# A decode kernel's layer norms: the columns centred only, the norm's factor applied behind the products, and x joined to the output amid w4's products

## The chip, the cores and the metric

The kernel runs on one core of one Trainium2 chip. The metric is device time in microseconds (us) of one execution; the time of a kernel is the median of its runs. Lower is better.

## The reference, cut to what matters

Two layers, each used twice: A is attention with a cache of keys and values for one new token, B a small network. Eight sequences (B = 8), width D = 448, 16 query heads on 8 key heads, 4096 cached positions, head width 256, hidden width F = 1792. All inputs are bf16.

```python
def _layernorm(x, axis=-1, eps=1e-5):
    m = jnp.mean(x, axis=axis, keepdims=True)
    v = jnp.var(x, axis=axis, keepdims=True)
    return (x - m) / jnp.sqrt(v + eps)

def _A_ref(x, k_cache, v_cache, wq, wo):
    q = (x @ wq).reshape(B, Sq, Hq, Dh).transpose(0, 2, 1, 3)
    ...                                   # k, v: each cache head serves two query heads
    p = _softmax(jnp.einsum("bhqd,bhkd->bhqk", q, k) * (Dh ** -0.5))
    o = jnp.einsum("bhqk,bhkd->bhqd", p, v)
    return o.transpose(0, 2, 1, 3).reshape(B, Sq, Hq * Dh) @ wo

def _B_ref(x, w1, w2, w3, w4):
    ...                                   # hs: four shifted parts of h, through w2
    x1 = x + hs
    h2 = _gelu(_layernorm(x1) @ w3) @ w4
    return x1 + h2

x = x + _A_ref(_layernorm(x), A_k_cache, A_v_cache, A_wq, A_wo)
x = x + _B_ref(_layernorm(x), B_w1, B_w2, B_w3, B_w4)
x = x + _A_ref(_layernorm(x), A_k_cache, A_v_cache, A_wq, A_wo)
x = x + _B_ref(_layernorm(x), B_w1, B_w2, B_w3, B_w4)
```

The sequence length is 1, so the four shifted parts of h are zero, hs is zero, and w1 and w2 play no part. B applied to a norm therefore holds two norms, one after the other: x1 is norm(x), and the columns for w3 are norm(norm(x)). Both have the same mean and variance behind them, so they differ by a factor per sequence.

## The kernel before

**The work.** Nearly all of the time goes into the caches: for each of two passes (the two uses of A), each sequence b and each pair of key heads gp, four blocks of keys and four of values of 1 MB each are loaded into one of 15 slots (`slots`, all parts of the tile `places`). A key block is transposed in place by VectorE (`transpose_k`, L713, three instructions), multiplied with the queries by TensorE (`scores`, L728), and the exponentials are taken by ScalarE (`exps`, L737). Values are multiplied by TensorE (`pv`, L783). Some blocks of the first pass stay in their slots for the second, some are parked in PSUM (`away`, `back`, L748 and L755). A key slot comes free when its scores are done, a value slot when its products are done; `emit_loads` then issues the next load on SP's queue, in an order fixed when the program is built.

**The order.** It is written out by hand (`manual_schedule`): one loop over the blocks (`items`), and in it, twice per block, `step(idx)`, which takes one piece of a generator that does the rest of the work of a sequence. A `yield` ends a piece. `add_gen` gives each generator the blocks between which it should run, and a number of pieces (`of`: 38 for `chain`, 23 for `rest`) by which `step` paces it. If the next pass needs a sequence's queries before its chain has ended, the loop takes pieces until they are there. On each engine the instructions run in the order in which they were written.

**The generators around the change.**

- `project_q(0, Bn, qT1)` runs alone at the start: the norm of all eight sequences, then the queries of the first pass with wq (L309). Its scratch is in `scratch`, that is, in the last slot.
- `chain(b)` follows the first pass of each sequence: output projection with wo (L358), `mlp(b, 1)` with w3 (L376) and w4 (L358), then `project_q(b, 1, qT)`, the queries of the second pass.
- `rest()` does the second pass's `mlp` for the first four sequences together.
- The last four sequences' second `mlp_hidden(MID, Bn - MID)` stands alone behind everything, followed by the output in rows: x goes through an identity into `o_row` in PSUM (L995, fp32, two matmuls of the trace for each in the program), the products with w4 are added to it (L1005), the sum is copied as bf16 (L1014) and stored (L1016).

**The norm.** x is held as columns, `xT`: 128 partitions x 4 blocks of D x sequences; the fourth block overlaps the third by 64 rows. `norm(x, nb, twice)` makes sums and sums of squares on VectorE (L220 to L223), adds over partitions with a matmul of ones (L228), copies the means (L231), makes the variance (L234, or L238 and L239), adds epsilon (L255, L261, L265), and lets GpSimd take the power -1/2 (`power`, L247). `twice` asks for two factors: `rs[:, 0]` for norm(x), `rs[:, 1]` for norm(norm(x)). For more than one sequence these are two instructions on GpSimd, the one for `rs[:, 1]` first. Then `xc` is x less its mean (L268), and `xb`, the bf16 columns for the products, is `xc` times the last factor (L276 and L284 for one sequence, three instructions of L286 for more: all rows of three blocks, and two halves of the fourth). With `twice`, x itself becomes x + norm(x) (L295, or L297 and L298).

**The gelu.** `mlp_hidden` halves the products out of PSUM (L394), makes the cubic (L395, L396), tanh on ScalarE (L397), and HT (L399), the columns for w4. In `project_q` the products are copied as they are (L318).

Of the kernel before, what the change touches and what calls it, by code (L numbers as in the profile page):

```python
# [11 lines left out]
ACT = mybir.ActivationFunctionType  # L12
ALU = mybir.AluOpType
EPS = 1e-5
# [3 lines left out]
def kernel(  # L18
# [27 lines left out]
    nc = tc.nc  # L46
    Bn, Sq, D = A_x.shape
# [10 lines left out]
    HC = F // 128  # L58
# [84 lines left out]
    low = consts.tile([128, 2, 4], FP32, name="low")  # L143
# [13 lines left out]
    def xbs(nb):  # L157
        return xb[1] if nb == 1 else xb[Bn][:, :, :nb]
# [18 lines left out]
    xT = consts.tile([128, 4, Bn], FP32, name="xT")  # L177
# [25 lines left out]
    def norm(x, nb, twice):  # L203

        def room(name, shape, at):
            n = shape[0] * shape[1]
            if nb < Bn:
                t = chn.tile([128, n * MID], FP32, tag=name)  # L210
                ap = t[:, 0 : n * nb]
            else:
                ap = scratch(at, n * nb)
            return ap.rearrange("p (s f b) -> p s f b", s=shape[0], f=shape[1])

        def bc(ap):
            return ap.unsqueeze(1).to_broadcast([128, 4, nb])

        xx = room("xx", (2, 4), 0)
        nc.vector.tensor_mul(xx[:, 0], x, wv[:].unsqueeze(2).to_broadcast([128, 4, nb]))  # L220
        nc.vector.tensor_mul(xx[:, 1], xx[:, 0], x)
        xs = room("xs", (1, 2), 512)[:, 0]
        nc.vector.tensor_reduce(  # L223
            xs, xx.rearrange("p s f b -> p s b f"), mybir.AxisListType.X, ALU.add
        )
        yield
        st = room_ps("st", nb).rearrange("p (s b) -> p s b", b=nb)
        nc.tensor.matmul(st, ones, xs, start=True, stop=True)  # L228
        yield
        mv = room("mv", (1, 2), 528)[:, 0]  # L230
        nc.vector.tensor_copy(mv, st)  # L231
        var = room("var", (1, 1), 608)[:, 0, 0]
        if nb == 1:
            nc.vector.scalar_tensor_tensor(  # L234
                var, mv[:, 0], mv[:, 0], mv[:, 1], ALU.mult, ALU.subtract, reverse1=True
            )
        else:
            nc.vector.tensor_mul(var, mv[:, 0], mv[:, 0])  # L238
            nc.vector.tensor_sub(var, mv[:, 1], var)  # L239


        ve = room("ve", (1, 2), 544)[:, 0]
        n = 2 if twice else 1
        rs = room("rs", (1, 2), 560)[:, 0]

        def power(k0, k1):
            nc.gpsimd.tensor_tensor(  # L247
                rs[:, k0:k1].rearrange("p n b -> p (n b)"),
                ve[:, k0:k1].rearrange("p n b -> p (n b)"),
                nhalf[:].to_broadcast([128, (k1 - k0) * nb]),  # L250
                ALU.pow,
            )

        if twice and nb == 1:
            nc.vector.scalar_tensor_tensor(  # L255
                ve[:, :, 0], var.to_broadcast([128, 2]), 0.0, eps2[:], ALU.max, ALU.add
            )
            power(0, 2)
        else:
            if twice:  # L260
                nc.vector.tensor_scalar(  # L261
                    ve[:, 1], var, 0.0, EPS * EPS / (1 + EPS), ALU.max, ALU.add
                )
                power(1, 2)
            nc.vector.tensor_scalar(ve[:, 0], var, 0.0, EPS, ALU.max, ALU.add)  # L265
            power(0, 1)
        xc = room("xc", (1, 4), 576)[:, 0]
        nc.vector.tensor_tensor(xc, x, bc(mv[:, 0]), ALU.subtract)  # L268
        yield
        if nb > 1:  # L270
            yield
        c = (1 + EPS) ** -0.5 if twice else 1.0
        rl = rs[:, n - 1]
        parts = ((0, 128, 0, 0, 3, 0), (0, 64, 64, 3, 4, 4), (64, 128, 64, 3, 4, 3))
        if nb == 1:
            nc.vector.scalar_tensor_tensor(  # L276
                xbs(1)[:, 0:4, 0], xc[:, :, 0], rl, low[:, int(twice)], ALU.mult, ALU.mult
            )
            parts = parts[1:2]
        for p0, p1, x0, f0, f1, to in parts:  # L280
            pp = slice(x0, x0 + p1 - p0)
            dst = xbs(nb)[p0:p1, to : to + f1 - f0, :]
            if nb == 1:
                nc.vector.tensor_scalar(dst, xc[pp, f0:f1], rl[pp], c, ALU.mult, ALU.mult)  # L284
            else:
                nc.vector.scalar_tensor_tensor(  # L286
                    dst,
                    xc[pp, f0:f1],
                    c,
                    rl[pp].unsqueeze(1).to_broadcast([p1 - p0, f1 - f0, nb]),  # L290
                    ALU.mult,
                    ALU.mult,
                )
        if twice and nb == 1:
            nc.vector.scalar_tensor_tensor(x, xc, rs[:, 0], x, ALU.mult, ALU.add)  # L295
        elif twice:
            nc.vector.tensor_tensor(xc, xc, bc(rs[:, 0]), ALU.mult)  # L297
            nc.vector.tensor_add(x, x, xc)  # L298
        yield

    def project_q(b0, nb, qT):

        yield from norm(xT[:, :, b0 : b0 + nb], nb, False)
        q_ps = room_ps("q", nb).rearrange("p (c b) -> p c b", b=nb)
        for j in range(2):
            for h in range(Hq):
                for fc in range(4):
                    w, xi = wblk(wq_sb, HD, 2 * h + j, fc)
                    nc.tensor.matmul(  # L309
                        q_ps[:, j * Hq + h, :],  # L310
                        w,
                        xbs(nb)[:, xi, :],
                        start=(fc == 0),
                        stop=(fc == 3),
                    )
                if h % 4 == 3:
                    yield
        nc.vector.tensor_copy(qT, q_ps)  # L318
        yield

    def spread_q(qT, qbd):
# [46 lines left out]

    def mlp_hidden(b0, nb):

        yield from norm(xT[:, :, b0 : b0 + nb], nb, True)
        h_ps = room_ps("h", nb)
        for c in range(HC):
            for fc in range(4):
                w, xi = wblk(w3_sb, F, c, fc)
                nc.tensor.matmul(  # L376
                    h_ps[:, c * nb : c * nb + nb],
                    w,
                    xbs(nb)[:, xi, :],
                    start=(fc == 0),  # L380
                    stop=(fc == 3),
                )
            if c % 4 == 3:
                yield
        yield
        g_t = chn.tile([128, 2, HC * MID], FP32, tag="g")
        hh, g0 = g_t[:, 0, 0 : HC * nb], g_t[:, 1, 0 : HC * nb]
        if nb == 1:
            HT_t = chn.tile([128, HC, 1], BF16, tag="HT")
            HT = HT_t[:]  # L390
        else:
            HT = HTw[:, :, b0 : b0 + nb]

        nc.vector.tensor_scalar_mul(hh, h_ps, 0.5)  # L394
        nc.vector.scalar_tensor_tensor(g0, hh, 2 * 0.044715, h_ps, ALU.mult, ALU.mult)  # L395
        nc.vector.scalar_tensor_tensor(g0, g0, 1.0, h_ps, ALU.add, ALU.mult)  # L396
        nc.scalar.activation(g0, g0, ACT.Tanh, scale=0.7978845608028654)  # L397
        yield
        nc.vector.scalar_tensor_tensor(  # L399
            HT,  # L400
            g0.rearrange("p (c b) -> p c b", b=nb),
            1.0,
            hh.rearrange("p (c b) -> p c b", b=nb),
            ALU.add,
            ALU.mult,
        )
        yield
        return HT

# [449 lines left out]
    for idx, it in enumerate(items):  # L859
        if idx == len(items) - 2:  # L860
            end = [slots[p] for p in places[:2]]
            ident2 = end[0][:, 0:256].bitcast(FP32)
            nc.vector.tensor_copy(ident2, identb[:])
            W = D // 4
            o_row = store[0][:, 0:W]
            nc.vector.memset(o_row, 0.0)
        n, kv, c = it
# [119 lines left out]
    xs = xT[:, :, MID:]  # L987
    nc.vector.tensor_add(xs, xs, st["y"])
    run(mlp_hidden(MID, Bn - MID))
    for q in range(4):  # L990
        for fc in range(4):
            at = min(128 * fc, D - 128)
            lo, hi = max(W * q, 128 * fc), min(W * q + W, at + 128)
            if lo < hi:
                nc.tensor.matmul(  # L995
                    o_row[32 * q : 32 * q + Bn, lo - W * q : hi - W * q],
                    xT[:, fc, :],
                    ident2[:, lo - at : hi - at],
                    start=(lo == W * q),
                    stop=False,  # L1000
                    skip_group_check=True,
                )
    for c in range(HC):
        for q in range(4):
            nc.tensor.matmul(  # L1005
                o_row[32 * q : 32 * q + Bn, :],
                HTw[:, c, :],
                w4_sb[:, c, W * q : W * q + W],
                start=False,
                stop=(c == HC - 1),  # L1010
                skip_group_check=True,
            )
# [36 lines left out]
```

## Time and profile before

| | |
|---|---|
| median of 3 runs | 1098.04 us |
| lowest and highest | 1095.36 and 1102.22 us |
| profiled execution: span | 1093.6 us |
| TensorE (PE) busy, weight loads (PEld) | 674.9 us, 451.8 us |
| VectorE (DVE) busy | 599.1 us |
| ScalarE (ACT), GpSimd (POOL) busy | 125.9 us, 16.3 us |
| mean rate of all transfers | 409 GB/s |
| read from HBM | 444.67 MB |
| mean granted clock of TensorE | 0.593 |

The span goes from the first to the last instruction of one profiled execution; the page gives no other time of that execution, so what lies around the span is seen only by comparing it with the runs. A line of the trace is read as start, length, engine, source line, operation, output and input, shapes, and in brackets how long the engine was idle before it and what ended that. SPq is SP's queue, on which the loads are issued. A busy share is an average over the whole execution: what a stretch is bound by is read from that stretch.

### The profile page before, as it was taken

What the parts mean: (1) busy time and instruction counts of PE and PEld (TensorE: products, weight loads), DVE (VectorE), ACT (ScalarE), POOL (GpSimd) and SP (SyncE); (2) the same over time, 40 slices, a digit from 0 to 9 for tenths busy, and PEclk for the clock granted to TensorE, in tenths of its full rate; (3) what the DMA queues carried; (4) which work ended last, traced back from release to release, by engine and by line L of the source; (5) the groups of instructions that cost most, each with busy time, mean ns of one, the idle gap of its engine ahead of it and who ended that gap; (6) DMA issues with size and microseconds to landing.
All of it is one profiled execution on the core that took longest, in us unless ns stands there. A gap on an engine that the chain in (4) does not pass through costs nothing. (4 is left out here: it accounts for less than half of the span.)

```text
span 1093.6 us, 32866 instructions
## 1 busy us (share of the span) xinstructions
PE 674.9 (62%) x15063; PEld 451.8 (41%) x15063; DVE 599.1 (55%) x1215; ACT 125.9 (12%) x362; POOL 16.3 (1%) x27
## 2 busy tenths in 40 slices
PE   3234568456864677446774467834776477767775
PEld 2123345334642355324552245522454244545554
DVE  4256564656366555555465564665637553585462
ACT  0001101110110111101021001201111101111110
POOL 0000000000000000000000000000000000000000
PEclk9986556655575556555566555665556555665565
DMA  9999999999999999999999999999999999999994
GB/s 356 394 427 419 416 403 420 420 416 407 418 423 419 406 417 422 423 419 402 419 422 423 420 401 418 423 421 417 411 416 421 420 398 419 421 411 409 421 417 188
DMA packets 62010, 446.80 MB, mean 409 GB/s; under 512 B 6568, under 2 KB 10544, under 8 KB 12336
## 3 DMA queue, kind: packets, MB, share of 16 engines
q1 hardware_dynamic: 61680, 444.32, 98.6%
q8 instruction: 118, 1.93, 0.7%
q10 hardware_dynamic: 192, 0.38, 0.2%
q14 instruction: 20, 0.16, 0.0%
HBM read 444.67 MB, written 0.01 MB: 407 GB/s over the span
## 5 line engine op out<-in xcount | busy, mean ns | idle before, releaser
L713 DVE STREAM_TRANSPOSE places<-places 128x512 uint32<-128x512 uint32 (+1 forms) x576 | 462.0, 858 | 263.1 <-DMA places<-in_A_k_cache_dram 262.7
L728 PE MATMUL sc<-places,qbd 128*8 128x128 bf16 (+1 forms) x6720 | 281.9, 309 | 217.8 <-DVE places L713 179.7
L783 PE MATMUL o<-places,ptw 128*8 128x256 bf16 x3968 | 241.9, 387 | 144.6 <-DMA places<-in_A_v_cache_dram 122.1
L728 PEld LDWEIGHTS <-qbd 128*8 128x8 bf16 x6720 | 161.2, 101 | 312.8 <-issue 136.8
L783 PEld LDWEIGHTS <-ptw 128*8 128x8 bf16 x3968 | 114.1, 109 | 192.2 <-issue 151.0
L737 ACT ACTIVATE p_n<-sc 128x256 bf16<-128x256 f32 x128 | 95.6, 747 | 763.1 <-PE sc L728 763.1
L309 PEld LDWEIGHTS <-wq_sb 128*128 128x128 bf16 x1152 | 36.0, 104 | 28.3 <-issue 18.4
L358 PEld LDWEIGHTS <-wo_sb 128*128 128x128 bf16 x1280 | 38.4, 102 | 19.8 <-issue 19.8
L332 DVE CAST qbd<-misc 32x64 bf16<-32x64 f32 x64 | 13.8, 216 | 55.6 <-PE misc L328 55.0
L309 PE MATMUL misc<-xb,wq_sb 128*128 128x1 bf16 x1024 | 34.5, 166 | 6.2 <-ACT ptw L771 3.2
L358 PE MATMUL misc<-OT,wo_sb 128*128 128x1 bf16 x1024 | 34.5, 165 | 1.2 <-issue 1.2
L737 ACT ACTIVATION_READ_ACCUMULATOR p_n<-sc 128x1 f32 x128 | 33.9, 265 | 0.0
L771 ACT CAST ptw<-misc 128x128 bf16<-128x128 f32 x64 | 17.4, 273 | 139.1 <-PE misc L764 79.1
L463 PEld LDWEIGHTS misc<-R,o_sb 128*128 128x128 f32 x124 | 26.1, 292 | 9.4 <-issue 8.6
L247 POOL TENSOR_TENSOR t<-t,nhalf 128x2 f32<-128x2 f32 (+2 forms) x20 | 14.0, 703 | 1064.9 <-DVE t L268 1064.9
L463 PE MATMUL misc<-R,o_sb 128*128 128x8 f32 x124 | 28.8, 342 | 0.1
L431 PE MATMUL misc<-zm,one 128*128 128x8 f32 (+1 forms) x66 | 18.5, 354 | 15.0 <-DVE zm L423 14.2
L755 DVE STREAM_TRANSPOSE places<-store 128x512 uint32<-128x512 uint32 x32 | 20.1, 684 | 10.7 <-PE sc L728 10.6
L431 PEld LDWEIGHTS misc<-zm,one 128*128 128x128 f32 x66 | 16.0, 300 | 21.5 <-issue 15.8
L376 PEld LDWEIGHTS <-w_sb 128*128 128x128 bf16 x560 | 17.2, 105 | 9.4 <-issue 9.2
L376 PE MATMUL misc<-xb,w_sb 128*128 128x1 bf16 (+1 forms) x560 | 18.5, 166 | 3.6 <-DVE xb L286 2.2
L748 DVE STREAM_TRANSPOSE store<-places 128x512 uint32<-128x512 uint32 x32 | 19.9, 690 | 0.9 <-DMA places<-in_A_v_cache_dram 0.8
(103 smaller groups left out, 241.9 us busy)
## 6 DMA issues: line engine op xcount, KB each, us to landing
places<-in_A_v_cache_dram SPq DMA_DIRECT2D x215, 1024.0 KB, 9.5
places<-in_A_k_cache_dram SPq DMA_DIRECT2D x146, 1024.0 KB, 9.9
places<-in_A_k_cache_dram SPq DMA_DIRECT2D x23, 2048.0 KB, 18.7
places<-in_A_v_cache_dram SPq DMA_DIRECT2D x8, 768.0 KB, 7.2
wo_sb<-in_A_wo_dram SPq DMA_DIRECT2D x1, 3584.0 KB, 27.5
wq_sb<-in_A_wq_dram SPq DMA_DIRECT2D x3, 1024.0 KB, 8.0
w_sb<-in_B_w_dram SPq DMA_DIRECT2D x1, 1568.0 KB
w_sb<-in_B_w_dram SPq DMA_DIRECT2D x3, 448.0 KB, 26.2
```

Source lines behind the costliest of these rows:

```text
L309: nc.tensor.matmul(q_ps[:, j * Hq + h, :], w, xbs(nb)[:, xi, :], start=(fc == 0), stop=(fc == 3),)
L358: nc.tensor.matmul(y_ps[:, fc, :], w[:, i, at : at + 128], rhs(i), start=start, stop=stop, skip_group_check=open is not None,)
L376: nc.tensor.matmul(h_ps[:, c * nb : c * nb + nb], w, xbs(nb)[:, xi, :], start=(fc == 0), stop=(fc == 3),)
L431: nc.tensor.matmul(z_ps, ones, zm[:], start=True, stop=True)
L463: nc.tensor.matmul(ot_ps[:, j], o_sb[:].rearrange("p (i j) -> p j i", j=2)[:, j], R[:], start=True, stop=True)
L713: nc.vector.transpose(w, w)
L728: nc.tensor.matmul(sc[32 * k : 32 * k + 8, 128 * x : 128 * (x + nx)], qbd[:, ep, gp].rearrange("p a h -> p (a h)"), v, start=(n == 0), sto ...
L737: nc.scalar.activation(p_sb[:, :, :, 2 * u : 2 * u + 2].rearrange("p t i x -> p x t i"), sc[:, 256 * u : 256 * u + 256].rearrange("p (x t ...
L748: nc.vector.transpose(store[n][:].bitcast(U32), slot[:].bitcast(U32)[:, 512 * n : 512 * n + 512])
L755: nc.vector.transpose(slot[:].bitcast(U32)[:, 512 * n : 512 * n + 512], store[n][:].bitcast(U32))
L771: nc.scalar.copy(ptw[:, :, :, 6:8], pt_ps.rearrange("p t k (a h) -> p a (t k) h", a=4),)
L783: nc.tensor.matmul(o_ps[32 * q : 32 * q + 8, :], ptz[:, at : at + 8], v[:, y * Dh : (y + 1) * Dh], start=False, stop=(y >= 12), skip_group ...
```

## The change

`norm` writes `xb` as soon as the means are there, as x less its mean without a factor, and ends a piece there; the variance and the powers follow in the next piece, at whose end `norm` returns. It returns the factor, and with `twice` also a function, `add_normed`, that makes x + norm(x); only for that is `xc` still made. A new function, `scaled`, applies the factor to the products when they are taken out of PSUM: in `project_q` in place of the copy, in `mlp_hidden` in place of the halving. The cubic is then made from the halved and scaled products in SBUF (with other constants) and not from the products in PSUM. `add_normed` runs after HT. A norm has three pieces instead of four (one sequence) or five (more); the paces are not changed. At the end, x's matmuls into `o_row` stand in front of the eighth of the 14 chunks of w4's products instead of before the first.

```diff
@@ norm
         mv = room("mv", (1, 2), 528)[:, 0]
         nc.vector.tensor_copy(mv, st)
+        parts = ((0, 128, 0, 0, 3, 0), (0, 64, 64, 3, 4, 4), (64, 128, 64, 3, 4, 3))
+        if nb == 1:
+            nc.vector.scalar_tensor_tensor(
+                xbs(1)[:, 0:4, 0], x[:, :, 0], mv[:, 0], low[:, 0], ALU.subtract, ALU.mult
+            )
+            parts = parts[1:2]
+        for p0, p1, x0, f0, f1, to in parts:
+            pp = slice(x0, x0 + p1 - p0)
+            dst = xbs(nb)[p0:p1, to : to + f1 - f0, :]
+            if nb == 1:
+                nc.vector.tensor_scalar(
+                    dst[:, :, 0], x[pp, f0:f1, 0], mv[pp, 0], None, ALU.subtract
+                )
+            else:
+                nc.vector.tensor_tensor(
+                    dst,
+                    x[pp, f0:f1],
+                    mv[pp, 0].unsqueeze(1).to_broadcast([p1 - p0, f1 - f0, nb]),
+                    ALU.subtract,
+                )
+        yield
         var = room("var", (1, 1), 608)[:, 0, 0]
...
-        xc = room("xc", (1, 4), 576)[:, 0]
-        nc.vector.tensor_tensor(xc, x, bc(mv[:, 0]), ALU.subtract)
-        yield
-        if nb > 1:
-            yield
...
-        yield
+        if twice:
+            xc = room("xc", (1, 4), 576)[:, 0]
+            nc.vector.tensor_tensor(xc, x, bc(mv[:, 0]), ALU.subtract)
+
+            def add_normed():
+                if nb == 1:
+                    nc.vector.scalar_tensor_tensor(x, xc, rs[:, 0], x, ALU.mult, ALU.add)
+                else:
+                    nc.vector.tensor_tensor(xc, xc, bc(rs[:, 0]), ALU.mult)
+                    nc.vector.tensor_add(x, x, xc)
+
+            return rs[:, 1], add_normed
+        return rs[:, 0]
+
+    def scaled(dst, ps, rs, factor, nb):
+
+        if nb == 1:
+            nc.vector.tensor_scalar(dst, ps, rs, factor, ALU.mult, ALU.mult)
+        else:
+            n = dst.shape[1]
+            nc.vector.scalar_tensor_tensor(
+                dst, ps, factor, rs.unsqueeze(1).to_broadcast([128, n, nb]), ALU.mult, ALU.mult
+            )
@@ project_q
-        nc.vector.tensor_copy(qT, q_ps)
+        scaled(qT, q_ps, rs, 1.0, nb)
@@ mlp_hidden
-        nc.vector.tensor_scalar_mul(hh, h_ps, 0.5)
-        nc.vector.scalar_tensor_tensor(g0, hh, 2 * 0.044715, h_ps, ALU.mult, ALU.mult)
-        nc.vector.scalar_tensor_tensor(g0, g0, 1.0, h_ps, ALU.add, ALU.mult)
-        nc.scalar.activation(g0, g0, ACT.Tanh, scale=0.7978845608028654)
+        scaled(
+            hh.rearrange("p (c b) -> p c b", b=nb),
+            h_ps.rearrange("p (c b) -> p c b", b=nb),
+            rs,
+            0.5 * (1 + EPS) ** -0.5,
+            nb,
+        )
+        nc.vector.scalar_tensor_tensor(g0, hh, 4 * 0.044715, hh, ALU.mult, ALU.mult)
+        nc.vector.scalar_tensor_tensor(g0, g0, 1.0, hh, ALU.add, ALU.mult)
+        nc.scalar.activation(g0, g0, ACT.Tanh, scale=2 * 0.7978845608028654)
         yield
         nc.vector.scalar_tensor_tensor(HT, ...)
+        add_normed()
         yield
@@ the output
+    def x_part():
+        ...                      # the loops over q and fc as before, with start=False
     for c in range(HC):
+        if c == HC // 2:
+            x_part()
         for q in range(4):
             nc.tensor.matmul(
                 o_row[32 * q : 32 * q + Bn, :],
                 HTw[:, c, :],
                 w4_sb[:, c, W * q : W * q + W],
-                start=False,
+                start=(c == 0),
                 stop=(c == HC - 1),
                 skip_group_check=True,
             )
```

More of the change, by code (lines that the diff above doesn't have):

```diff
@@ L266, in norm @@
             power(0, 1)
-        xc = room("xc", (1, 4), 576)[:, 0]
-        nc.vector.tensor_tensor(xc, x, bc(mv[:, 0]), ALU.subtract)
-        yield
-        if nb > 1:
-            yield
-        c = (1 + EPS) ** -0.5 if twice else 1.0
-        rl = rs[:, n - 1]
-        parts = ((0, 128, 0, 0, 3, 0), (0, 64, 64, 3, 4, 4), (64, 128, 64, 3, 4, 3))
+        if twice:
[10 more added lines that the diff above has]
+    def scaled(dst, ps, rs, factor, nb):
         if nb == 1:
+            nc.vector.tensor_scalar(dst, ps, rs, factor, ALU.mult, ALU.mult)
+        else:
+            n = dst.shape[1]
             nc.vector.scalar_tensor_tensor(
-                xbs(1)[:, 0:4, 0], xc[:, :, 0], rl, low[:, int(twice)], ALU.mult, ALU.mult
+                dst, ps, factor, rs.unsqueeze(1).to_broadcast([128, n, nb]), ALU.mult, ALU.mult
             )
[L279 to L298, printed above, removed]
-        yield
     def project_q(b0, nb, qT):
-        yield from norm(xT[:, :, b0 : b0 + nb], nb, False)
+        rs = yield from norm(xT[:, :, b0 : b0 + nb], nb, False)
         q_ps = room_ps("q", nb).rearrange("p (c b) -> p c b", b=nb)
@@ L369, in mlp_hidden @@
     def mlp_hidden(b0, nb):
-        yield from norm(xT[:, :, b0 : b0 + nb], nb, True)
+        rs, add_normed = yield from norm(xT[:, :, b0 : b0 + nb], nb, True)
         h_ps = room_ps("h", nb)
@@ L989 @@
     run(mlp_hidden(MID, Bn - MID))
[L990 to L1002, printed above, removed]
+    def x_part():
+        for q in range(4):
+            for fc in range(4):
+                at = min(128 * fc, D - 128)
+                lo, hi = max(W * q, 128 * fc), min(W * q + W, at + 128)
+                if lo < hi:
+                    nc.tensor.matmul(
+                        o_row[32 * q : 32 * q + Bn, lo - W * q : hi - W * q],
+                        xT[:, fc, :],
+                        ident2[:, lo - at : hi - at],
+                        start=False,
+                        stop=False,
+                        skip_group_check=True,
+                    )
     for c in range(HC):
+        if c == HC // 2:
+            x_part()
         for q in range(4):
```

## The prediction

> **What bounds the kernel now.** I read the page first, then the kernel cut into stretches of 10 us, then the end and the start in order of time, then the waits. "Faster" and "slower" below mean by over 1%, 11 us here: the three runs shown spread over 0.6%, so less than about 1% can hardly be told from no change. First the page's head, its engine row and its DMA rows:
>
> ```profile
> span 1093.6 us, 32866 instructions
> PE 674.9 (62%) x15063; PEld 451.8 (41%) x15063; DVE 599.1 (55%) x1215; ACT 125.9 (12%) x362; POOL 16.3 (1%) x27
> DMA  9999999999999999999999999999999999999994
> DMA packets 62010, 446.80 MB, mean 409 GB/s; under 512 B 6568, under 2 KB 10544, under 8 KB 12336
> ```
>
> No compute engine is above 62%; the DMA engines are at nine tenths or more in 39 of 40 slices, and the change touches no transfer. Next, three of the 10 us stretches (PE, PEld, DVE, ACT and POOL busy, then granted clock, DMA share, GB/s):
>
> ```profile
> 630.00:640.00 10.00, 8.22 (x170) 5.71 (x170) 5.71 (x13) 1.29 (x4) 0.00 (x0) 0.50 0.98 387
> ...
> 1070.00:1080.00 10.00, 7.60 (x230) 6.82 (x229) 1.62 (x10) 1.05 (x3) 0.00 (x0) 0.50 0.87 354
> 1080.00:1090.00 10.00, 5.12 (x152) 4.50 (x153) 3.46 (x21) 0.25 (x1) 1.99 (x2) 0.50 0.01 2
> ```
>
> The first is one of the poorest in the middle: even there the DMA share is 0.98, against 1.01 in the stretch 60 to 1080 us as a whole, at 416 GB/s. So compute is exposed only after the last load lands, at about 1080.7 us. That tail, in order of time (start, length, engine, line, idle time before it and what ended it):
>
> ```profile
> 1083.77 0.17 DVE L231 COPY t<-misc 128x8 f32<-128x8 f32 x1 [0.69 <-PE misc L228]
> ...
> 1084.36 0.17 DVE L261 TENSOR_SCALAR t<-t 128x4 f32<-128x4 f32 x1
> ...
> 1084.67 1.99 POOL L247 TENSOR_TENSOR t<-t,nhalf 128x4 f32<-128x4 f32 x2 [67.88 <-DVE t L268]
> 1085.72 0.55 DVE L286 SCALAR_TENSOR_TENSOR xb<-t 128x12 bf16<-128x12 f32 x3 [1.05 <-POOL t L247]
> 1085.95 1.74 PE L376 MATMUL misc<-xb,w_sb 128*128 128x4 bf16 x56 [2.22 <-DVE xb L286]
> ...
> 1087.62 0.58 PE L995 MATMUL store<-places,xT 128*8 128x112 f32 x14
> 1087.72 0.22 DVE L394 TENSOR_SCALAR g_t<-misc 128x56 f32<-128x56 f32 x1 [0.64 <-PE misc L376]
> ...
> 1088.75 0.22 DVE L399 SCALAR_TENSOR_TENSOR HTw<-g_t 128x56 bf16<-128x56 f32 x1 [0.32 <-ACT g_t L397]
> 1089.02 1.48 PE L1005 MATMUL store<-w_sb,HTw 128*8 128x112 bf16 x56 [0.83 <-DVE HTw L399]
> 1090.55 0.27 DVE L1014 CAST places<-store 128x112 bf16<-128x112 f32 x1 [1.59 <-PE store L1005]
> ```
>
> From the means (L231) to the products with w3 (L376) lie 2.2 us, nearly half of it GpSimd's first power. The x part (L995) runs while VectorE and ScalarE make the gelu, so it costs nothing now.
>
> **The change in the tail.** The sum is against the profiled execution's span, 1093.6 us, the only time of its own that the page has; the median of the runs, 1098.04, lies 4.4 us above it, and I carry the difference over.
>
> Products start earlier. The three centring operations follow L231 at once, at 1083.96 where the variance starts now. The three of L286 that they replace began 0.19 us apart, and PE started 0.23 us after the first (1085.72 to 1085.95), so PE now starts at 1084.19. It needs 1.77 us to VectorE's next start (1085.95 to 1087.72), plus about 0.1 us, once, for the half block that the second operation writes at about 1084.3: the products are done at about 1086.05.
>
> The factor comes later. The variance is pushed back by three operations, 3 x 0.19 = 0.57 us, so the first power starts at 1084.67 + 0.57 = 1085.24. From its start to VectorE's use 1.05 us passed (1084.67 to 1085.72), so the factor is there at 1086.29. Of the two, this is the later. The new scaling operation thus starts at 1086.29 and not, like L394, at 1087.72: 1.43 us gained. What replaces the wait for the power before the products is a wait of 0.24 us for it behind them. Behind it on VectorE stand the two operations of the cubic and HT; ScalarE waits for them.
>
> Scaling and gelu keep four operations on VectorE. The new form of the first (two tensor inputs, one from PSUM, 56 elements) is in no row of before as such; L395 has two tensor inputs, one from PSUM, at 0.214 us, L394 has one at 0.196. I take +0.02 us; its bounds are 0 and, by L318's 0.425 us for 256 elements, +0.2.
>
> The cubic's operations now run beside the second power. In this trace the three operations of L286, with two tensor inputs from SBUF, also ran under the second power, in 0.157 to 0.172 us each, against 0.162 for the same line's 64-row form at the start with GpSimd idle: no contention, and I take none. Against that stands the Trainium skill, GPSIMD Engine Reference, section Specifications: GpSimd's SBUF interface is shared with VectorE, and VectorE operations with two SBUF inputs contend for it. By that page the cubic would be held from 1086.54 to the power's end at about 1087.25, and the tail's sum would be -0.1 us instead of the one below.
>
> The x part moves onto the path. Its 14 matmuls took 0.58 us hidden under the gelu; now they stand after 28 of w4's 56 and lengthen that stretch by as much: +0.58 us (bounds +0.4 if weight loads overlap, +0.65). Its new input comes from two operations after HT: these are L297 and L298, 0.40 us from the first's start to the second's end, and need the second power, done at 1085.24 + 1.99 = 1087.23. HT ends at about 1087.57, x at about 1088.0; PE comes to the x part at 1087.62 + 28 x 0.0268 = 1088.37. So x has 0.37 us to spare; without that cover the wait would be added one for one.
>
> Sum: -1.43 + 0.02 + 0.58 = -0.83 us.
>
> **The change at the start.** The first projection loses its wait for the power (1.64 us on GpSimd), but the next rows show that the products wait for wq:
>
> ```profile
> 7.80 0.57 DVE L286 SCALAR_TENSOR_TENSOR xb<-places 128x24 bf16<-128x24 f32 x3 [1.67 <-POOL places L247]
> 9.54 0.19 PE L309 MATMUL store<-xb,wq_sb 128*128 128x8 bf16 x1 [4.31 <-DMA wq_sb<-in_A_wq_dram]
> ```
>
> The columns were ready at 8.4 us; ready at 6.1 they gain nothing. The factor now stays in scratch, which lies in the last cache slot, until the scaling at 18.15 us; SP fills that slot after eight other loads behind w4's issue at 29.8 us, so nothing on SP's queue is held.
>
> **The change in the middle.** Per batch element there is one norm with two factors and one with one. Operations on VectorE stay the same in the first and fall by one (L268, 0.154 us) in the second. VectorE no longer stops for GpSimd ahead of the columns. The generators have two steps fewer per chain, while the pace (38) stays, so their pieces move ahead by one or two half items among transposes, scores and pv; SP's order of loads stays. The waits that matter (total us, times, longest):
>
> ```profile
> DVE places L713 <- DMA places<-in_A_k_cache_dram: 262.7, 118, 18.5
> DVE qT L318 <- PE misc L309: 25.6, 8, 6.0
> DVE xb L276 <- POOL t L247: 5.3, 8, 0.7
> ```
>
> The transposes are what SP's next loads wait for through the scores, and VectorE idles 262.7/118 = 2.2 us on average for the data ahead of them: that cover hides what the chains do. Bounds: at best, the 5.3 us of waits and 8 x 0.154 = 1.2 us all come off the transfers, -6.5 us; at worst, each of eight chains gets a wait like L318's (25.6/8 = 3.2 us) at a new place, 1.0 us past the cover, +8 us. I take 0, by the DMA share: an engine set that is busy all the time has no gap to give back, and a 1 us shift does not open one.
>
> **Rivals.** (a) The moved pieces starve the transfers. The wait of VectorE for a chain's last product (L318, now the scaling, which waits for the factor too) comes to stand before a landed key block at its longest, 6.0 us; past the 2.2 us of cover that is 3.8 us in each of eight chains: 30 - 0.8, or 1127 us. It decides from about 1.5 us past the cover in every chain (8 x 1.5 = 12). For it: stretches such as 630 to 640 fall to 387 GB/s when chain work is dense. Against: even those have a share of 0.98, and 2 fewer steps of 38 hardly gather the work.
>
> (b) The middle gains. If chains off VectorE's way lifted the mean of 416 GB/s to the 421 that many stretches show, 1020 us would become 1008: 1085 us. For it: the poor stretches lie near the chains. Against: the poorest (630 to 640) is ahead of any norm, at the output projection, which is unchanged.
>
> (c) The scaling waits for both powers, which GpSimd does one after the other: it starts 1.99 - 1.01 = 0.98 us later (the powers' row, and the chain's 1.01 for the first alone), and the tail loses -0.83 + 0.98 = +0.15 us: 1098.2. For it: both are issued together and stand in one tile. Against: L286 started at the first one's end. This is the change not doing what it says, and on the clock it is not told from the forecast.
>
> **How the numbers follow.** Forecast (with (c), both within 1%) 0.93, of it 0.80 for the tail's -0.8 and 0.13 for (c); (a) 0.04; (b) 0.03. Time: 1098.04 - 0.83 = 1097.2 us. Bounds of the middle give 1097.2 - 6.5 = 1090.7 and 1097.2 + 8 = 1105.2; the upper end asks a late chain of all eight, so I stop at 1103, which leaves out (a) and (b).
>
> **What would show it.** In the changed profile the first product with w3 in the tail should start about 0.4 us after the copy of the means (2.2 now); scaling should be released by GpSimd about 2.5 us after that copy (L394: 3.95); the x part should stand within w4's products without a wait for x; from the last load's landing to the end about 0.8 us less than the 12.9 of now (1093.6 - 1080.7). Up to there, the DMA share should stay at 1.01 and the rate near 416 GB/s. A last landing later than 1086 or earlier than 1074 us would prove the middle step wrong; a scaling that starts later than 1086.5, or a pause before the x part, the tail's.

## The result, and the profile after

The changed kernel takes 1106.8 us (median of nine runs; 1101.8 to 1111.8) beside 1098.5 us for the kernel before (nine runs; the 1098.04 above is of three of them): ratio 1.0069, 95% interval 1.0046 to 1.0092. It is slower by about 8 us, where the prediction had 0.8 us less. Its profiled execution has a span of 1105.3 us, 11.7 more than before. The head of the profile's page, its engine row and its DMA rows:

```profile
span 1105.3 us, 32851 instructions
PE 679.7 (61%) x15063; PEld 455.6 (41%) x15063; DVE 596.5 (54%) x1206; ACT 125.3 (11%) x362; POOL 16.4 (1%) x27
DMA  9999999999999999999999999999999999999995
DMA packets 62010, 446.80 MB, mean 404 GB/s; under 512 B 6568, under 2 KB 10544, under 8 KB 12336
```

VectorE has less to do (596.5 against 599.1 us), the bytes are the same, and the DMA row still shows nines. Only the mean rate fell, from 409 to 404 GB/s.

**The tail did what was forecast.** In order of time, as for the kernel before, whose own first line here is the products with its last values:

```profile
1080.76 0.59 PE L797 MATMUL store<-ptw,places 128*128 128x2 bf16 x16 [0.65 <-DMA places<-in_A_v_cache_dram]
```

And the changed kernel:

```profile
1093.48 0.58 PE L815 MATMUL store<-ptw,places 128*128 128x2 bf16 x16 [0.66 <-DMA places<-in_A_v_cache_dram]
...
1096.48 0.17 DVE L231 COPY t<-misc 128x8 f32<-128x8 f32 x1 [0.69 <-PE misc L228]
1096.68 0.55 DVE L246 TENSOR_TENSOR xb<-xT,t 128x12 bf16<-128x12 f32 x3
1096.90 1.74 PE L387 MATMUL misc<-xb,w_sb 128*128 128x4 bf16 x56 [0.46 <-DVE xb L246]
...
1097.97 1.99 POOL L268 TENSOR_TENSOR t<-t,nhalf 128x4 f32<-128x4 f32 x2 [68.48 <-DVE t L290]
1099.02 0.22 DVE L308 SCALAR_TENSOR_TENSOR g_t<-misc,t 128x56 f32<-128x56 f32 x1 [1.05 <-POOL t L268]
1099.27 0.22 DVE L412 SCALAR_TENSOR_TENSOR g_t<-g_t 128x56 f32<-128x56 f32 x1
...
1100.33 0.83 PE L1027 MATMUL store<-w_sb,HTw 128*8 128x112 bf16 x28 [1.68 <-DVE HTw L416]
...
1100.94 0.59 PE L1014 MATMUL store<-places,xT 128*8 128x112 f32 x14
1101.31 0.87 PE L1027 MATMUL store<-w_sb,HTw 128*8 128x112 bf16 x28
1102.23 0.27 DVE L1036 CAST places<-store 128x112 bf16<-128x112 f32 x1 [1.66 <-PE store L1027]
```

From the products with the last values to the last copy (L1036, L1014 before) it takes 1102.23 - 1093.48 = 8.75 us, against 1090.55 - 1080.76 = 9.79: 1.04 us less. So nearly 13 us were lost before the tail between these two executions. By the medians it is about 9 us (8.3 and the tail's 1.0): the span profiled before, 1093.6 us, is that of one of its fastest runs.

**The loss lies in the stretches where a chain runs.** One such stretch, before and then after (last three columns: granted clock, DMA share, GB/s):

```profile
250.00:260.00 10.00, 7.24 (x170) 4.82 (x174) 6.53 (x16) 1.08 (x4) 0.70 (x1) 0.50 1.00 408
260.00:270.00 10.00, 6.37 (x154) 4.25 (x150) 6.02 (x14) 0.89 (x3) 0.00 (x0) 0.50 1.01 411
```

```profile
250.00:260.00 10.00, 7.55 (x186) 5.12 (x178) 6.33 (x16) 0.74 (x2) 0.70 (x1) 0.50 0.97 366
260.00:270.00 10.00, 7.01 (x172) 4.44 (x164) 6.22 (x15) 1.13 (x4) 0.00 (x0) 0.50 1.00 370
```

The rate falls by a tenth while the share reads 0.97 and 1.00. The share is thus no proof that the transfers have nothing to give. Adding up the bytes moved, the changed kernel falls behind by 1 to 2 us in seven of the eight chains, by nothing in one, and by little between them. Single executions scatter, though: "Products early, scaling and the rest in their old places" (below), which is as fast as the kernel before, also has 367 GB/s in the first of these two stretches (415 in the second). What the loss is worth is therefore taken from the medians, and its cause from the order of time and the experiments.

What is new there stands in the waits of the changed kernel (total us, times, longest):

```profile
PE misc L782 <- DVE g_t L305: 5.6, 8, 0.7
```

L782 is TensorE's transposition of the exponentials (`transpose_p`), which stands between the two halves of a key block's scores; L305 is the scaling of w3's products. The kernel before has no such wait. In order of time, one block of one chain, in the changed kernel:

```profile
260.82 2.43 DVE L731 STREAM_TRANSPOSE places<-places 128x1024 uint32<-128x1024 uint32 x3 [2.42 <-DMA places<-in_A_k_cache_dram]
262.12 0.60 PE L746 MATMUL sc<-places,qbd 128*8 128x128 bf16 x16 [1.44 <-DVE places L731]
263.18 0.19 DVE L305 TENSOR_SCALAR g_t<-misc,t 128x14 f32<-128x14 f32 x1
...
263.42 0.27 PE L782 MATMUL misc<-identb,p_n 128*128 128x32 bf16 x4 [0.70 <-DVE g_t L305]
...
263.62 0.60 PE L746 MATMUL sc<-places,qbd 128*8 128x128 bf16 x16
...
264.26 0.33 SPq L718 DMA_DIRECT2D places<-in_A_k_cache_dram  x1
```

The key block lands; VectorE transposes it; its first 16 scores are done at 262.7 us. Then TensorE stands for 0.70 us, because the transposition follows the scaling in the program, and the scaling stands on VectorE behind the key's own transposes. Only when the second half of the scores is through does SP issue the slot's next load: 3.44 us after the landing. In the kernel before, the same block has the transposition at once behind the first 16 scores, and nothing there waits for the halving (L394):

```profile
256.81 2.43 DVE L713 STREAM_TRANSPOSE places<-places 128x1024 uint32<-128x1024 uint32 x3 [1.93 <-DMA places<-in_A_k_cache_dram]
258.11 0.60 PE L728 MATMUL sc<-places,qbd 128*8 128x128 bf16 x16 [0.77 <-DVE places L713]
258.64 0.29 PE L764 MATMUL misc<-identb,p_n 128*128 128x32 bf16 x4
258.86 0.82 PE L728 MATMUL sc<-places,qbd 128*8 128x128 bf16 x16
...
259.31 0.17 DVE L394 TENSOR_SCALAR g_t<-misc 128x14 f32<-128x14 f32 x1
...
259.73 0.33 SPq L700 DMA_DIRECT2D places<-in_A_k_cache_dram  x1
```

From landing to the next load that is 2.92 us. In this block of all eight chains the trace of the changed kernel has 3.44 us, that of the kernel before 2.91.

**Why half a microsecond matters.** The chain of waits of the kernel before, read in a stretch in the middle and not as a sum, shows it:

```profile
1000.40 6.97 DMA places<-in_A_k_cache_dram
1007.36 0.02 issue
1007.39 2.44 DVE places L713 x3
1009.83 0.04 issue
1009.87 0.41 PE sc L728 x8
1010.28 0.02 issue
1010.30 7.37 DMA places<-in_A_k_cache_dram
```

It is a ring: a key load takes about 7.2 us from issue to landing, its transposes 2.4, the scores 0.4 behind them, and then the load that waited for this slot is issued. One turn lasts 9.9 to 10.4 us here. In that time two key and two value blocks pass, 4.19 MB, and 4.19 MB in 10.3 us are 407 GB/s: near the 404 to 417 GB/s of the chains' stretches in the kernel before. Here a release sets the next landing, and what delays the scores comes on top.

### The profile page after: what moved, and what is told of

It reads as the page before. It is cut to its first block, busy times and chain, and to the rows that moved or that the text cites. A ratio compares the mean times of both kernels' runs of the same rounds, so it can differ in the third digit from the quotient of the medians.

```text
span 1105.3 us, 32851 instructions
## 1 busy us (share of the span) xinstructions
PE 679.7 (61%) x15063; PEld 455.6 (41%) x15063; DVE 596.5 (54%) x1206; ACT 125.3 (11%) x362; POOL 16.4 (1%) x27
## 5 line engine op out<-in xcount | busy, mean ns | idle before, releaser
L481 PEld LDWEIGHTS misc<-R,o_sb 128*128 128x128 f32 x124 | 28.1, 314 | 10.3 <-issue 9.4
L782 PE MATMUL misc<-identb,p_n 128*128 128x32 bf16 x256 | 17.7, 188 | 6.2 <-DVE g_t L305 5.6
```

The costliest lines, as they stand in the source:

```text
L481: nc.tensor.matmul(ot_ps[:, j], o_sb[:].rearrange("p (i j) -> p j i", j=2)[:, j], R[:], start=True, stop=True)
L782: nc.tensor.matmul(pt_ps[:, t], p_sb[:, t].rearrange("p i x -> p (i x)"), cols, start=True, stop=True,)
```

## The experiments

Theory A: the places of the pieces cost; A1, of these, the scaling's place ahead of a transposition. Theory B: the arithmetic costs (the factor comes later, the scaling waits for it). All ratios are to the kernel before, run beside each experiment (median 1098.7 us in the first four, 1099.7 in the next four, 1099.5 in the last four), with 95% intervals; a ratio can differ from that of the two medians by up to 0.0015.

**All pieces restored.** The change, with `norm` ending as many pieces as before:

```diff
-            return rs[:, 1], add_normed
-        return rs[:, 0]
+            yield
+            if nb > 1:
+                yield
+            return rs[:, 1], add_normed
+        yield
+        return rs[:, 0]
```

Expected: 

> The change with the norm's pieces restored: a piece ends after the powers (two for more than one sequence), so that the products start in the same piece as before the change; the arithmetic is that of the change. Theory A (the loss lies in the places of the pieces: with two pieces fewer per chain the scaling of w3's products stands ahead of a key block's scores, and TensorE waits for it there): the loads run as before, and only the tail's 1.0 us is left of the change: ratio 0.999, about 1097.5 us, and TensorE's waits for the scaling (5.6 us in eight) are gone. Theory B (the loss lies in the arithmetic: the scaling waits for the products and GpSimd, the factor comes later): still 1.006 to 1.008, about 1106 us.

Measured: 1100.1 us, ratio 1.0004 (0.9983 to 1.0025). The waits for the scaling are gone. The loss is gone with them, although all of the arithmetic is there: theory B, with 1.006 to 1.008, falls. The gain of the tail did not show.

**Pieces joined in the kernel before.** Here w3's and wq's columns are scaled as before, but the products follow them in the same piece:

```diff
-        if nb > 1:
-            yield
...
             nc.vector.tensor_add(x, x, xc)
-        yield
```

Expected: 

> The kernel before, with the norm's last piece joined to the first piece of the products, and the extra piece for more than one sequence taken out, so that the chains have as many pieces as with the change; the arithmetic, the gelu and the tail are those of before. Theory A: the loss of the middle shows without the change's arithmetic, 12 us: ratio about 1.010, 1110 us, and TensorE waits for the halving (L394 before) ahead of a transposition of the exponentials. Theory B: 1.000, 1098.5 us.

Measured: 1117.5 us, ratio 1.0158 (1.0128 to 1.0189). None of the change's arithmetic is in it, and it is slower still. It has the wait behind the gelu, and a second one besides, since the columns and their products now both stand ahead of a key block's scores. Here are the two blocks of one chain in order of time, and then the total of the wait behind the gelu (L393 is its cubic):

```profile
255.85 2.43 DVE L710 STREAM_TRANSPOSE places<-places 128x1024 uint32<-128x1024 uint32 x3 [1.26 <-DMA places<-in_A_k_cache_dram]
...
258.44 0.73 PE L373 MATMUL misc<-xb,w_sb 128*128 128x1 bf16 x16 [3.62 <-DVE xb L274]
...
259.10 1.02 PE L725 MATMUL sc<-places,qbd 128*8 128x128 bf16 x32
...
260.17 0.33 SPq L697 DMA_DIRECT2D places<-in_A_k_cache_dram  x1
...
260.80 2.43 DVE L710 STREAM_TRANSPOSE places<-places 128x1024 uint32<-128x1024 uint32 x3 [1.90 <-DMA places<-in_A_k_cache_dram]
...
263.75 0.27 PE L761 MATMUL misc<-identb,p_n 128*128 128x32 bf16 x4 [0.89 <-DVE g_t L393]
...
264.60 0.33 SPq L697 DMA_DIRECT2D places<-in_A_k_cache_dram  x1
```

```profile
PE misc L761 <- DVE g_t L393: 7.6, 8, 1.1
```

TensorE idles 3.62 us for columns that stand on VectorE behind the key's transposes, and the scores wait behind these products. From landing to the next load the two blocks take 4.32 and 3.80 us (to within 0.01 in all eight chains) where 2.91 is usual: late by 2.3 us a chain, 18 us in eight, and 1.0158 is 17 us. So the run confirms theory A, and here the lateness of the releases accounts for the loss; its size is that of two waits, and it is no copy of the change's order.

**The change in the tail alone.** The old `norm` and `mlp_hidden` serve everything but the last four sequences; these take the new ones, with x amid w4's products:

```diff
...
-    run(mlp_hidden(MID, Bn - MID))
+    run(mlp_hidden_late(MID, Bn - MID))
...
```

Expected: 

> The change in the last norm and gelu alone (the four last sequences behind all loads, and x amid w4's products); everything before it is the kernel before. Both theories: the loads run as before and the tail is 1.0 us shorter: ratio 0.999, 1097.5 us, last product of w4's end 9.8 - 1.0 = 8.8 us after the last values' first product. If the tail of the change gave nothing, 1.000.

Measured: 1096.8 us, ratio 0.9978 (0.9957 to 0.9998); a second measurement follows below.

**Pieces restored in w3's norms alone.**

```diff
-            return rs[:, 1], add_normed
+            yield
+            if nb > 1:
+                yield
+            return rs[:, 1], add_normed
```

Expected: 

> The change with the pieces restored in the norms for w3 alone; the norms for wq keep one piece fewer. Theory A with all of the loss at w3's scaling: ratio 0.999, as with all pieces restored; with half of it at each norm: 1.003 to 1.004, about 1102 us. Theory B: 1.006 to 1.008, about 1106 us.

Measured: 1099.7 us, ratio 1.0010 (0.9987 to 1.0033). The piece that wq's norms lost costs nothing that could be told; most of the loss belongs to w3's (half of it at each, 1.003 to 1.004, lies at the interval's very end).

**Products early, scaling and the rest in their old places.** One piece more (two for several sequences) between the loop of products and the scaling:

```diff
             if c % 4 == 3:
                 yield
         yield
+        yield
+        if nb > 1:
+            yield
```

Expected: 

> The change with one piece more between w3's products and the scaling (two for more than one sequence): the products stay a half block early, as with the change; scaling, gelu, w4's products and the rest go back to where they stood before. Theory A1 (what costs is the scaling ahead of a key block's scores, where TensorE's transposition of the exponentials waits for it): 1.000 to 1.001, about 1099 us, and no waits of that transposition for the scaling. Theory A2 (what costs is where w3's products stand): about as with the change, 1.006, 1105 us.

Measured: 1099.8 us, ratio 0.9999 (0.9980 to 1.0018); no waits for the scaling. Where the products stand costs nothing that could be told.

**Products, scaling and gelu early, w4's products in their old places.** The same lines behind `add_normed()`:

```diff
         add_normed()
         yield
+        yield
+        if nb > 1:
+            yield
```

Expected: 

> The change with one piece more behind HT (two for more than one sequence): products, scaling and gelu stay a half block early, w4's products and what follows go back to where they stood before. Theory A1: the waits of the transposition for the scaling stay (5.6 us in eight), and most of the loss with them: 1.004 to 1.007, about 1104 us. Theory A3 (what costs is where w4's products stand): 1.000 to 1.001, about 1099 us.

Measured: 1104.5 us, ratio 1.0049 (1.0029 to 1.0070). The 5.6 us of waits are there, and so is the loss. These two kernels differ in the place of scaling and gelu, with the x + norm(x) behind them, alone.

**More work on TensorE in the kernel before.** w3's first four chunks are multiplied three times in one piece of each chain:

```diff
-        for c in range(HC):
+        seen = 0
+        for c in [0, 1, 2, 3] * (2 if nb == 1 else 0) + list(range(HC)):
...
-            if c % 4 == 3:
+            seen = seen + 1
+            if c % 4 == 3 and seen > (8 if nb == 1 else 0):
                 yield
```

Expected: 

> The kernel before, with w3's first four chunks of products made three times in each of the eight chains: 32 matmuls, 1.0 us on TensorE, more per chain in one piece, with the same result. If the loads run with cover to spare, as the prediction had it: 1.000, 1098.5 us. If in these stretches a slot's release sets when its next load lands, so that time on TensorE between a landing and a release comes back in the period of the loads: up to 8 x 1.0 us, ratio 1.004 to 1.007, 1103 to 1106 us.

Measured: 1102.7 us, ratio 1.0032 (1.0010 to 1.0054), below the 1.004 to 1.007 of full exposure. In the chain at 250 us the piece takes 1.86 us for 64 products where 32 took 1.01, so some 7 us were put on TensorE in eight chains, and 3.5 came back in the time (1.1 to 5.9). TensorE's time is not hidden in these stretches, and not all of it is exposed either: these products stood behind the scores of a block, ahead of the products with values.

**One piece later, not earlier.** Two pieces behind the powers of w3's norm for one sequence:

```diff
+            yield
+            yield
             return rs[:, 1], add_normed
```

Expected: 

> The change with two pieces more (not one) behind the powers of w3's norm for one sequence: everything from w3's products on stands a half block later than before the change, not earlier. If the place within a block decides (ahead of a key block's scores, or behind them), this is as bad as the change: the transposition waits for the scaling again, 1.005 to 1.008, about 1105 us. If it is being early that costs, or having few pieces: 1.000 to 1.001, about 1099 us.

Measured: 1099.4 us, ratio 1.0002 (0.9984 to 1.0021). The premise of the expectation was wrong: `step` does not take a piece at each of its two calls, and the added piece did not move the gelu ahead of the next block. The trace has the scaling behind a whole block of scores and no wait of the transposition for it:

```profile
260.24 0.82 PE L748 MATMUL sc<-places,qbd 128*8 128x128 bf16 x16
...
261.50 0.23 DVE L307 TENSOR_SCALAR g_t<-misc,t 128x14 f32<-128x14 f32 x1 [0.88 <-PE misc L389]
```

No wait, no loss: that agrees with A1, but tells nothing on being late.

**The wait taken away, the pieces left.** In the changed kernel, the transposition is written ahead of the piece:

```diff
-            step(idx)
             turn = None
             if c == TURN(n) and n - 1 in p_of:
-                turn = lambda t=p_of.pop(n - 1): transpose_p(t)
+                transpose_p(p_of.pop(n - 1))
+            step(idx)
```

Expected: 

> The change with all its pieces where they are; only the transposition of the exponentials, which stood between the two halves of a key block's scores, is written ahead of the piece that comes before the scores, so that it no longer follows the scaling. Theory A1 (that wait is what costs): the 5.6 us of waits are gone, and with them most of the loss: 1.000 to 1.002, about 1100 us. If the wait is a sign only and the places of the products or w4's chunks cost: 1.005 to 1.007, about 1105 us.

Measured: 1101.3 us, ratio 1.0001 (0.9980 to 1.0022). The same block in this kernel:

```profile
258.16 0.27 PE L782 MATMUL misc<-identb,p_n 128*128 128x32 bf16 x4
258.18 2.43 DVE L731 STREAM_TRANSPOSE places<-places 128x1024 uint32<-128x1024 uint32 x3 [2.16 <-DMA places<-in_A_k_cache_dram]
...
259.48 0.98 PE L746 MATMUL sc<-places,qbd 128*8 128x128 bf16 x24 [1.05 <-DVE places L731]
260.53 0.19 DVE L305 TENSOR_SCALAR g_t<-misc,t 128x14 f32<-128x14 f32 x1
260.66 0.39 PE L746 MATMUL sc<-places,qbd 128*8 128x128 bf16 x8 [0.21 <-DVE places L731]
...
261.09 0.33 SPq L718 DMA_DIRECT2D places<-in_A_k_cache_dram  x1
```

From landing to the next load 2.91 us again. The scaling stands where it stood in the change; only what waited for it was moved out of its way. TensorE still waits in this block, but elsewhere, behind the scores and ahead of w4's products:

```profile
PE misc L369 <- DVE HT_t L416: 4.8, 8, 0.6
```

There a wait of nearly the same size costs nothing that could be told. What costs is the wait that stands between a key block's landing and its slot's release.

**The same step in the kernel before, as a control.** Expected: 

> The kernel before with the same step: the transposition of the exponentials ahead of the piece before the scores. A control: no wait for a halving is there to be taken away, so 0.999 to 1.001, 1098 to 1100 us, unless the new place of the transposition gains or costs by itself.

Measured: 1099.7 us, ratio 0.9993 (0.9975 to 1.0010): the transposition's new place by itself neither gains nor costs anything that could be told.

**The tail's change with that step.** Expected: 

> The change in the last norm and gelu alone, with the transposition of the exponentials ahead of the piece: the tail's 1.0 us and what the control shows of the transposition's place: 0.998 to 1.000, about 1097.5 us.

Measured: 1097.1 us, ratio 0.9982 (0.9959 to 1.0006).

**The tail's change alone, again.** Expected: 

> The change in the last norm and gelu alone, once more beside the others: 0.998 to 0.9995 (the tail is 1.0 us shorter, 0.999), about 1097.5 us.

Measured: 1099.3 us, ratio 0.9986 (0.9968 to 1.0003). With 0.9978 the first time, it is among the lowest measured: about 0.2% below the kernel before, half of which the tail's 1.0 us explains. The first interval just excludes no change and the second just includes it.

## Why the prediction was wrong, point by point

- The tail was right. Products started 0.42 us after the copy of the means (forecast 0.42), the scaling 2.54 us (2.52), released by GpSimd. The cubic's operations, with two inputs in SBUF, ran in 0.22 us each and 0.25 us apart beside the second power; before, with GpSimd idle and one input in PSUM, they took 0.21 us and stood as far apart, and HT, with two inputs in SBUF, took 0.22. No contention shows, so for operations of this size the measurement decides against the rule of the Trainium skill (GPSIMD Engine Reference, section Specifications) that was weighed there; that section speaks of contention, and that the cubic would be held to the power's end was the prediction's own reading. The x part waited for nothing, but was mis-sized: the stretch from w4's first product to the copy grew from 1.53 to 1.90 us, so 0.37 for a forecast 0.58, just under the lower bound given (0.4). Hence -1.04 and not -0.83 us.
- The start was right: up to 130 us both kernels have moved the same bytes to within 0.3 us.
- The step that failed is the one on the middle: "I take 0, by the DMA share: an engine set that is busy all the time has no gap to give back, and a 1 us shift does not open one." The share stayed at 0.97 to 1.00 where the rate fell from 408 to 366 GB/s, and a delay of 0.53 us in one block of each chain did cost time. The worst case drawn up for the middle, +8 us, was of the right size, but came from VectorE's waits, and the range was then cut at 1103 us.
- The cover was the wrong one. VectorE's 2.2 us of idle time ahead of the transposes do not hide anything on the way from a landing to a release: VectorE idles there because the next block lands late, and it lands late because the slot was released late. TensorE's wait behind the scaling was not in the list of what waits for what, since only VectorE's waits were priced. That one place makes the release of one key slot per chain 0.53 us late (3.44 against 2.91).
- Rival (a) had the direction and the neighbourhood (chain pieces that move ahead among the scores) but named VectorE's wait for a product, not TensorE's wait for VectorE, and was set aside by the DMA share. "2 fewer steps of 38 hardly gather the work" missed that a piece need not be gathered, only put on the wrong side of a block's scores. Rival (b) called 630 to 640 the poorest stretch; 370 to 380 and 500 to 510 are poorer (382 and 381 GB/s), and they too lie ahead of their chain's norm.
- Open is the size: 8 x 0.53 = 4.2 us is what the key slots' releases are late by. From the change to the kernel with the wait taken away it is 1.0069 - 1.0001, about 7.5 us, good to some 3 us either way. Whether the rest is scatter, the runs do not settle. w4's chunks, which also stand earlier in the change (1.0069 with them, 1.0049 without, intervals that overlap), are not likely to be it: in the kernel with the wait taken away they are as early, and the value slot's next load is issued as late after the key block's landing (4.98 us there, 5.01 in the change, 3.77 before), at a ratio of 1.0001. Why the transposition waits for a scaling that reads other columns of the tile `misc` was not tried.

## What to carry to other kernels

Where loads go into slots that come free one at a time, follow one slot around (issue, landing, first use, last use, next issue) in the chain of waits before believing a busy DMA row: if the next issue follows the release at once, everything between landing and release is on the path, on whatever engine. In an order written out by hand, taking a step away moves all that follows; look at what each moved operation now stands ahead of, and who, on another engine, waits for it. And a gain in a tail is best put into the tail alone: the same edit in the body moved an order that had been right.

## What the runs showed of the hardware that was not expected

The DMA share was 0.97 and 1.00 at 366 and 370 GB/s, and 1.00 to 1.02 at 408 to 424 GB/s, with the same blocks loaded: here the share of busy time hardly told a full rate from one a tenth lower. Fourteen fp32 matmuls that by themselves spanned 0.58 us added only 0.37 us when they were put among bf16 matmuls.
